# Masked scores in another pool, Q's banks read engine by engine, small copies on POOL, K copies on SP

## The chip, the core and the metric

The kernel runs on one core of one Trainium2 chip. The metric is the device time of one execution in microseconds (us); lower is better. The core has five queues that matter here: TensorE (PE; its weight loads are listed as PEld), VectorE (DVE), ScalarE (ACT), GpSimd (POOL) and SyncE (SP). Each runs its own instructions in order; across queues they wait by semaphores. DMAs are issued from POOL's queue or from SP's and carried out by 16 DMA engines.

## What is computed

Three blocks follow each other. The first is attention within chunks of 64 tokens (batch 8, 8 heads, 576 tokens, head size 64). The second mixes each token with the one before it and applies a gated two-layer network (512 to 1024 to 512). The third, the only one that the change touches, is causal attention by four experts with head size 64, of which each token takes the best two:

```
logits = x @ w_gate
topk, w = best 2 of 4 logits, softmax over these two
for e in range(4):
    q, k, v = x @ wq[e], x @ wk[e], x @ wv[e]          # (8, 576, 64)
    scores = where(causal, -1e9, q @ k.T / sqrt(64))
    a = softmax(scores)
    ye = a @ v @ wo[e]
    out += (weight of e for each token) * ye
```

## The kernel before

Every product is made from three matmuls on values split into a high and a low part (`mm3`, lines 57 to 59): high x high, high x low, low x high. High parts are rounded copies made by ScalarE, low parts the difference, made by VectorE; both read the same bank of PSUM.

The mix stage (`attn_mix`) works in units of 384 tokens. Its last unit ends with `mix_v`: the product goes through line 289 (times the gate, into `x2o`), line 46 (high half, POOL), line 292 (low half, VectorE) and line 293 (store of both, `x2T<-x2d`, POOL's queue) to memory in HBM. Its weights and buffers lie in the pools `wts` and `mx`.

The expert stage (`experts`) starts before the mix stage has ended: ahead of the last eight half products of `mix_v`, lines 768 to 794 load the first batch and make its projections; these use the pools `pX`, `wB`, `sB` (lines 469 to 472), which lie on memory that the mix stage has given back by then (`wkr`). Line 796 yields; what follows it comes later in the program. There the pools `yB`, `wB2` and `psT` are opened (lines 797 to 799): `yB` and `wB2` lie on the memory of `wts` and `mx`. The kernel's queues are put in order by a planner, which simulates the program and lets an instruction that comes earlier in the program go first where both are ready; of a pool it queues nothing ahead of the last users of the pools whose memory that pool takes.

For each batch b and pair of experts p, `p_qk` makes K and Q for both experts at once, in two halves of 288 tokens (h = 0, 1): K is split (lines 528, 529) into `Kph` and `Kpl`, and six DMAs (lines 534, 535) copy it into `K` (the high part twice, in both halves of the partitions) and `Kl`. Q is split per expert i into one tile `Q`: the high part in the expert's half of the partitions (line 518), the low part in the other half (line 519). The last 64 tokens go into `Ql` (lines 522, 523), block diagonal, so that the last, short tile of both experts runs as one. `p_v4` makes V and the gate logits of the last tile for two batches, `p_v` those of the four full tiles. All of these use two banks of PSUM in turn (tag `pj`).

A step (`t_S`, line 603) makes the scores of one tile of 128 queries into a bank (tag `S`, two banks); line 624 masks and scales them into `sm` and writes the row extreme into `nm`; line 634 takes the exponential into `P`. Three steps later `t_T` transposes `P` (line 682) and splits it into `PTh` and `PTl` (lines 688, 689, pool `wB2`); four steps later `t_AV` multiplies with V. Nine steps make a pair, 18 a batch. K and Q of the next pair are made between the steps (`fill`), in the steps 1 to 4 and 9 to 12 of a batch, and are queued behind the step's last score matmul. `t_scale` sends the row sums through HBM (lines 664 to 669, SP's queue), line 731 on POOL multiplies, line 742 splits, and `t_out` writes the output (lines 757, 760, SP's queue).

Of the kernel before, what the change touches and what calls it, by code (L numbers as in the profile page):

```python
# [8 lines left out]
F32 = mybir.dt.float32  # L9
F32R = mybir.dt.float32r  # L10
I32 = mybir.dt.int32
ACTF = mybir.ActivationFunctionType
ALU = mybir.AluOpType
# [35 lines left out]
def f32(ap):  # L49
    return ap.bitcast(F32)  # L50
# [399 lines left out]
def experts(tc, at_pool, weights, out, x2T, w_gate, wq, wk, wv, wo, ident, dram, B, S):  # L450
# [3 lines left out]
    nc = tc.nc  # L454
    E, DM, D = wq.shape
    KD = DM // 128
    EP = E // 2
    HB = S // 2
# [3 lines left out]
    LT = NT - 1  # L462
    SF = LT * 128
# [4 lines left out]
    with ExitStack() as ctx:  # L468
        px = ctx.enter_context(tc.tile_pool(name="pX", bufs=1, side="right", reuse_waits="tile"))
        wts = ctx.enter_context(tc.tile_pool(name="wB", bufs=1, side="right", reuse_waits="tile"))  # L470
        sb = ctx.enter_context(tc.tile_pool(name="sB", bufs=2, side="right", reuse_waits="tile"))
# [31 lines left out]
        def p_qk(b, p, nm, h):  # L503
            ws = w_q if nm == "Q" else w_k
            cc = slice(h * HB, (h + 1) * HB)
            pc = slice(p * 128, (p + 1) * 128)
            pp = ps.tile([128, DM], F32, tag="pj", bufs=CFG["ps"][3], name="pj")[:, :HB]
            x = x2[b]
            mm3(nc, pp, [((ws[g][0][:, pc], ws[g][1][:, pc]), (x.hi[:, g, cc], x.lo[:, g, cc])) for g in range(KD)])
            two = (b * EP + p) % 2  # L510
            if nm == "Q":
                n = min(SF, cc.stop) - cc.start
                c = slice(cc.start, cc.start + n)
                for i in range(2):
                    if h == 0:
                        Q[b, 2 * p + i] = px.tile([128, SF], F32R, tag="Q", bufs=CFG["qb"], name="Q")
                    t = Q[b, 2 * p + i]
                    nc.scalar.activation(out=t[half[i], c], in_=pp[half[i], :n], func=ACTF.Copy)
                    nc.vector.tensor_tensor(t[half[1 - i], c], pp[half[i], :n], f32(t[half[i], c]), op=ALU.subtract)
                    if n < HB:  # L520
                        d = QL[two][half[i], :, half[i]]
                        nc.scalar.activation(out=d[:, 0], in_=pp[half[i], n:], func=ACTF.Copy)
                        nc.vector.tensor_tensor(d[:, 1], pp[half[i], n:], f32(d[:, 0]), op=ALU.subtract)
                return
            if h == 0:
                K[b, p] = [px.tile([128, S], F32R, tag="Kp" + x, bufs=CFG["kp"], name="Kp" + x) for x in "hl"]
            t, l = K[b, p]
            nc.scalar.activation(out=t[:, cc], in_=pp, func=ACTF.Copy)  # L528
            nc.vector.tensor_tensor(l[:, cc], pp, f32(t[:, cc]), op=ALU.subtract)
            if h == 1:  # L530
                for i in range(2):
                    KD2[b, 2 * p + i] = d = px.tile([128, SF], F32R, tag="K", bufs=CFG["qb"], name="K")
                    for j in range(2):
                        nc.gpsimd.dma_start(out=d[half[j]], in_=t[half[i], :SF])  # L534
                    nc.gpsimd.dma_start(out=KL[two][i][half[i]], in_=l[half[i], :SF])


        V4s = [sb.tile([128, E, 2, D], F32R, bufs=1, name=f"V4{i}") for i in range(3)]
# [3 lines left out]
        def p_v4(b):  # L542

            x = sb.tile([128, 2, KD, 2, 64], F32R, tag="x0", bufs=1, name="x0")
            for i in range(2):
                for j in range(2):
                    nc.gpsimd.dma_start(out=x[:, i, :, j], in_=x2T[b // 2][i, :, j * S + SF:(j + 1) * S]
                                        .rearrange("(g p) t -> p g t", p=128))
            xh, xl = (x[:, i].rearrange("p g j t -> p g (j t)") for i in range(2))
            pp = ps.tile([128, DM], F32, tag="pj", bufs=CFG["ps"][3], name="pj")[:, :NV]  # L550
            mm3(nc, pp, [((xh[:, g], xl[:, g]), (w_v[g][0][:, :NV], w_v[g][1][:, :NV])) for g in range(KD)])
            for j in range(2):
                V4[b + j] = v = V4s[(b + j) % 3]
                G[b + j] = g = sb.tile([128, NT, E], F32, tag="lg", bufs=3, name="lg")
                r = half[j]
                pv = pp[r, :E * D].rearrange("p (e d) -> p e d", e=E)
                nc.scalar.activation(out=v[:64, :, 0], in_=pv, func=ACTF.Copy)
                nc.scalar.activation(out=v[64:, :, 0], in_=pv, func=ACTF.Copy)
                nc.vector.tensor_tensor(v[:64, :, 1], pv, f32(v[:64, :, 0]), op=ALU.subtract)
                for k in half:  # L560
                    nc.vector.tensor_copy(g[k, LT], pp[r, E * D:])

        def p_v(b, m):
            if m == 0:
                V[b] = sb.tile([128, LT, E, 2, D], F32R, tag="V", bufs=2, name="V")
            s, n = tiles[m]
            x, v = x2[b], V[b][:, m]
            pp = ps.tile([128, DM], F32, tag="pj", bufs=CFG["ps"][3], name="pj")[:, :NV]
# [34 lines left out]
        def t_S(b, p, t, i):  # L603

            s = tiles[t][0]
            nk = s + tiles[t][1]
            sm = yb.tile([128, S], F32, tag="sm", bufs=CFG["sm"], name="sm")
            nm = sb.tile([128, 2], F32, tag="nm", bufs=CFG["sm"], name="nm")
            if t < LT:
                e = 2 * p + i  # L610
# [308 lines left out]
```

## Time and profile before

| | |
|---|---|
| median of 3 runs | 1038.33 us (1037.39 to 1039.74) |
| profiled execution | 1040.81 us, its span 1038.9 us |
| mean granted TensorE clock | 0.976 of full speed |
| TensorE busy (weight loads) | 976.5 us, 94% (933.5 us, 90%) |
| VectorE, ScalarE, POOL busy | 672.6 us (65%), 577.4 us (56%), 428.1 us (41%) |
| DMA | 108.38 MB, mean 104 GB/s |

The first 120 us load the inputs and split weights; up to 656 us the mix stage keeps TensorE busy; from there to the end the expert stage runs. Busy time says when an engine had an instruction in work, the granted clock how fast TensorE was let run, and a bracket behind an instruction in a list in order of time says how long its engine was idle before it and which engine, tile and line it waited for. Matmuls overlap, so the distance of their starts, not their duration, is their pace.

### The profile page before, as it was taken

Reading aid. Unit: us, or ns where it says so; the run is one execution under the profiler, and the core shown is the slowest. Engines: PE = TensorE matmul, PEld = TensorE weight load, DVE = VectorE, ACT = ScalarE, POOL = GpSimd, SP = SyncE. Lnnn points to the kernel's source line nnn. Section 1 sums busy time; section 2 is a strip of 40 time slices with the busy share of each in tenths; the row PEclk is TensorE's granted clock in tenths of the full one; section 3 lists DMA queues with packets and bytes.
Section 4 is the critical chain, followed back from the end, with each engine's and each line's share of the span. In section 5 each row is a group of like instructions: output and inputs, shape, how many; then the busy total and the mean of one; then the engine's idle time right before and its main releaser. Section 6 shows DMA issues by size and latency. Waiting matters only on the chain.

```text
span 1038.9 us, 21755 instructions
## 1 busy us (share of the span) xinstructions
PE 976.5 (94%) x8214; PEld 933.5 (90%) x8214; DVE 672.6 (65%) x1686; ACT 577.4 (56%) x1355; POOL 428.1 (41%) x535
## 2 busy tenths in 40 slices
PE   2669899999999999999999999799999999999997
PEld 2569899999999999999999999789899899989986
DVE  5899935437654755564557432478876877877886
ACT  3478573545354645454444413266766767676665
POOL 5444303526453645464554436424342333433211
PEclk8789999999999999999999999989999999999999
DMA  8784423152324252333123124553555546353512
GB/s 223 188 198 133 118 67 82 41 122 55 90 55 110 62 122 46 98 74 91 52 52 79 35 62 117 96 154 84 163 110 151 154 95 184 74 163 72 167 32 103
DMA packets 170079, 108.38 MB, mean 104 GB/s; under 512 B 134024, under 2 KB 146424, under 8 KB 169976
## 3 DMA queue, kind: packets, MB, share of 16 engines
q1 hardware_dynamic: 132024, 54.55, 20.4%
q0 software_dynamic: 37952, 52.45, 19.6%
q8 instruction: 65, 1.06, 0.4%
q14 instruction: 38, 0.31, 0.1%
HBM read 66.01 MB, written 28.38 MB: 91 GB/s over the span
## 4 chain that ended last, share of the span: by engine, by line
PE 74%; DVE 13%; ACT 6%; DMA 3%; issue 2%; POOL 1%; SPq 1%; DVEq 0%; ACTq 0%; POOLq 0%
PE mps L57 14%; PE mps L59 13%; PE mps L58 13%; PE pj L57 6%; PE pj L59 6%; PE pj L58 6%; PE Sps L622 4%; PE Tps L127 3%; PE Tps L682 3%; PE AVps L715 2%; PE AVps L711 2%; DVE sm L624 1%; DVE PTl L689 1%; PE Sps L154 1%; DMA st<-in_moe_w_k_dram 1%
## 5 line engine op out<-in xcount | busy, mean ns | idle before, releaser
L57 PE MATMUL mps<-xhk,wkh 128*128 128x384 f32 x384 | 132.7, 347 | 2.0 <-DVE r L270 1.9
L58 PE MATMUL mps<-xlk,wkh 128*128 128x384 f32 x384 | 129.6, 338 | 0.0
L59 PE MATMUL mps<-xhk,wkl 128*128 128x384 f32 x384 | 129.4, 337 | 0.0
L57 PE MATMUL mps<-kh,wvh 128*128 128x384 f32 x384 | 129.3, 341 | 0.1
L58 PE MATMUL mps<-kl,wvh 128*128 128x384 f32 x384 | 127.7, 335 | 0.1
L59 PE MATMUL mps<-kh,wvl 128*128 128x384 f32 x384 | 126.9, 336 | 0.9 <-DVE wvl L325 0.9
L274 POOL TENSOR_TENSOR kl<-r,kh 128x384 fp32r<-128x384 f32 x80 | 86.0, 1079 | 80.4 <-ACT kh L273 80.1
L270 DVE TENSOR_TENSOR r<-mps,r 128x384 f32<-128x384 f32 x80 | 44.3, 554 | 99.9 <-ACT r L267 99.7
L634 ACT ACTIVATE P<-sm,nm 128x512 f32<-128x512 f32 (+3 forms) x144 | 83.9, 584 | 26.1 <-DVE nm L624 14.6
L228 POOL TENSOR_TENSOR xa<-XT 128x384 f32<-128x384 f32 x72 | 68.2, 955 | 62.7 <-DVE xlr L244 37.1
L624 DVE CUSTOM_DVE_ANT_0 sm<-Sps,mask 128x256 f32<-128x256 f32 (+4 forms) x160 | 74.7, 477 | 15.3 <-PE Sps L622 13.9
L689 DVE TENSOR_TENSOR PTl<-Tps,PTh 128x512 fp32r<-128x512 f32 (+2 forms) x144 | 70.7, 504 | 7.9 <-ACT PTh L688 6.9
L57 PEld LDWEIGHTS mps<-xhk,wkh 128*128 128x128 f32 x384 | 72.9, 190 | 3.0 <-DVE r L270 2.5
L242 DVE SCALAR_TENSOR_TENSOR xa<-xa,mu,XT 128x384 f32<-128x384 f32 x72 | 63.7, 900 | 15.0 <-POOL xa L228 14.9
L534 POOL DMA_DIRECT2D K<-Kph x64 | 34.5, 553 | 93.6 <-ACT Kph L528 59.2
L59 PEld LDWEIGHTS mps<-kh,wvl 128*128 128x128 f32 x384 | 71.8, 188 | 1.2 <-DVE wvl L325 1.2
L58 PEld LDWEIGHTS mps<-xlk,wkh 128*128 128x128 f32 x384 | 72.7, 189 | 0.1
L57 PEld LDWEIGHTS mps<-kh,wvh 128*128 128x128 f32 x384 | 72.0, 188 | 0.8 <-DVE x2o L289 0.4
L59 PEld LDWEIGHTS mps<-xhk,wkl 128*128 128x128 f32 x384 | 72.6, 189 | 0.0
L58 PEld LDWEIGHTS mps<-kl,wvh 128*128 128x128 f32 x384 | 72.1, 188 | 0.4 <-POOL kl L274 0.4
L273 ACT ACTIVATE kh<-r 128x384 fp32r<-128x384 f32 x96 | 50.9, 530 | 38.0 <-DVE r L270 36.9
L57 PE MATMUL mps<-xhr,wrh 128*128 128x384 f32 x192 | 66.6, 349 | 4.6 <-ACT sig L257 3.3
(188 smaller groups left out, 2855.3 us busy)
## 6 DMA issues: line engine op xcount, KB each, us to landing
x2T<-x2d POOLq DMA_DIRECT2D x48, 384.0 KB, 3.2
x<-x2T POOLq DMA_DIRECT2D x32, 576.0 KB, 6.4
ldv<-in_v_dram SPq DMA_DIRECT2D x144, 64.0 KB
ldq<-in_q_dram SPq DMA_DIRECT2D x32, 256.0 KB
ldk<-in_k_dram SPq DMA_DIRECT2D x32, 256.0 KB
K<-Kph POOLq DMA_DIRECT2D x64, 128.0 KB, 2.8
out_dram<-o SPq DMA_DIRECT2D x32, 256.0 KB
st<-in_moe_w_k_dram SPq DMA_DIRECT2D x8, 512.0 KB
```

Of the source, the lines that this page charges most:

```text
L57: nc.tensor.matmul(out=out, lhsT=ah, rhs=bh, start=first and i == 0, stop=False)
L58: nc.tensor.matmul(out=out, lhsT=ah, rhs=bl, start=False, stop=False)
L59: nc.tensor.matmul(out=out, lhsT=al, rhs=bh, start=False, stop=last and i == n - 1)
L228: nc.gpsimd.tensor_tensor(d, now, prev, op=ALU.subtract)
L242: nc.vector.scalar_tensor_tensor(a, d, m, prev, op0=ALU.mult, op1=ALU.add)
L270: nc.vector.tensor_tensor(r2, p, r, op=ALU.mult)
L273: nc.scalar.activation(out=o.hi, in_=r2, func=ACTF.Copy)
L274: eng(nc, CFG["klo"][u >= CFG["nearly"]]).tensor_tensor(o.lo, r2, f32(o.hi), op=ALU.subtract)
L622: issued = nc.tensor.matmul(out=pp[:, :w], lhsT=x, rhs=y[:, a:a + w], start=n == 0, stop=n == len(terms) - 1)
L624: nc.vector.tensor_tensor_reduce(out=sm[:, a:a + w], in0=pp[:, :w], in1=mk[:, :w], op0=ALU.add, op1=ALU.min, scale=-scale, scalar=3e38, ac ...
L634: nc.scalar.activation(out=x[:, :nk], in_=sm[:, :nk], func=ACTF.Exp, scale=-1.0, bias=nm[:, :1], accum_out=z)
L689: nc.vector.tensor_tensor(l, src, f32(h), op=ALU.subtract)
```

## The change

In the expert stage six things are done otherwise. `sm` is taken from the pool `sB` in place of `yB`. V of odd batches is taken from `yB` in place of `sB`, with one buffer in each pool in place of two in `sB`. A bank of Q is read by ScalarE for both experts and then by VectorE for both, over all its 288 columns; the tile `Q` grows from 512 to 576 columns. The remainder `Ql` is copied from `Q` by four POOL instructions in place of two by ScalarE and two by VectorE from the bank. The six copies of K are issued by SP in place of POOL. In `p_v4` the second high copy of V (line 558) and the second copy of the gate logits (line 560) go to POOL, from the first ones.

```diff
--- before.py
+++ after.py
@@ -509,18 +509,18 @@
             mm3(nc, pp, [((ws[g][0][:, pc], ws[g][1][:, pc]), (x.hi[:, g, cc], x.lo[:, g, cc])) for g in range(KD)])
             two = (b * EP + p) % 2
             if nm == "Q":
-                n = min(SF, cc.stop) - cc.start
-                c = slice(cc.start, cc.start + n)
-                for i in range(2):
-                    if h == 0:
-                        Q[b, 2 * p + i] = px.tile([128, SF], F32R, tag="Q", bufs=CFG["qb"], name="Q")
-                    t = Q[b, 2 * p + i]
-                    nc.scalar.activation(out=t[half[i], c], in_=pp[half[i], :n], func=ACTF.Copy)
-                    nc.vector.tensor_tensor(t[half[1 - i], c], pp[half[i], :n], f32(t[half[i], c]), op=ALU.subtract)
-                    if n < HB:
-                        d = QL[two][half[i], :, half[i]]
-                        nc.scalar.activation(out=d[:, 0], in_=pp[half[i], n:], func=ACTF.Copy)
-                        nc.vector.tensor_tensor(d[:, 1], pp[half[i], n:], f32(d[:, 0]), op=ALU.subtract)
+                if h == 0:
+                    for i in range(2):
+                        Q[b, 2 * p + i] = px.tile([128, S], F32R, tag="Q", bufs=CFG["qb"], name="Q")
+                ts = [Q[b, 2 * p + i] for i in range(2)]
+                for i, t in enumerate(ts):
+                    nc.scalar.activation(out=t[half[i], cc], in_=pp[half[i]], func=ACTF.Copy)
+                for i, t in enumerate(ts):
+                    nc.vector.tensor_tensor(t[half[1 - i], cc], pp[half[i]], f32(t[half[i], cc]), op=ALU.subtract)
+                if h == 1:
+                    for i, t in enumerate(ts):
+                        for j in range(2):
+                            nc.gpsimd.tensor_copy(QL[two][half[i], j, half[i]], f32(t[half[i ^ j], SF:]))
                 return
             if h == 0:
                 K[b, p] = [px.tile([128, S], F32R, tag="Kp" + x, bufs=CFG["kp"], name="Kp" + x) for x in "hl"]
@@ -531,8 +531,8 @@
                 for i in range(2):
                     KD2[b, 2 * p + i] = d = px.tile([128, SF], F32R, tag="K", bufs=CFG["qb"], name="K")
                     for j in range(2):
-                        nc.gpsimd.dma_start(out=d[half[j]], in_=t[half[i], :SF])
-                    nc.gpsimd.dma_start(out=KL[two][i][half[i]], in_=l[half[i], :SF])
+                        nc.sync.dma_start(out=f32(d[half[j]]), in_=f32(t[half[i], :SF]))
+                    nc.sync.dma_start(out=f32(KL[two][i][half[i]]), in_=f32(l[half[i], :SF]))
 
 
         V4s = [sb.tile([128, E, 2, D], F32R, bufs=1, name=f"V4{i}") for i in range(3)]
@@ -555,14 +555,14 @@
                 r = half[j]
                 pv = pp[r, :E * D].rearrange("p (e d) -> p e d", e=E)
                 nc.scalar.activation(out=v[:64, :, 0], in_=pv, func=ACTF.Copy)
-                nc.scalar.activation(out=v[64:, :, 0], in_=pv, func=ACTF.Copy)
                 nc.vector.tensor_tensor(v[:64, :, 1], pv, f32(v[:64, :, 0]), op=ALU.subtract)
-                for k in half:
-                    nc.vector.tensor_copy(g[k, LT], pp[r, E * D:])
+                nc.vector.tensor_copy(g[r, LT], pp[r, E * D:])
+                nc.gpsimd.tensor_copy(v[64:, :, 0], f32(v[:64, :, 0]))
+                nc.gpsimd.tensor_copy(g[half[1 - j], LT], g[r, LT])
 
         def p_v(b, m):
             if m == 0:
-                V[b] = sb.tile([128, LT, E, 2, D], F32R, tag="V", bufs=2, name="V")
+                V[b] = (yb if b % 2 else sb).tile([128, LT, E, 2, D], F32R, tag="V", bufs=1, name="V")
             s, n = tiles[m]
             x, v = x2[b], V[b][:, m]
             pp = ps.tile([128, DM], F32, tag="pj", bufs=CFG["ps"][3], name="pj")[:, :NV]
@@ -604,7 +604,7 @@
 
             s = tiles[t][0]
             nk = s + tiles[t][1]
-            sm = yb.tile([128, S], F32, tag="sm", bufs=CFG["sm"], name="sm")
+            sm = sb.tile([128, S], F32, tag="sm", bufs=CFG["sm"], name="sm")
             nm = sb.tile([128, 2], F32, tag="nm", bufs=CFG["sm"], name="nm")
             if t < LT:
                 e = 2 * p + i
```

## Rows read from the trace of the kernel before

**Rows 1.** Busy time by stretch: length, busy us of each engine (instructions), granted clock, DMA share, GB/s
```profile
656.50:700.00 43.50, 36.44 (x253) 34.36 (x251) 26.45 (x99) 23.82 (x68) 14.73 (x28) 0.92 0.55 135
676.50:682.30 5.80, 5.80 (x25) 5.76 (x26) 1.57 (x7) 2.62 (x8) 1.52 (x4) 0.50 0.50 144
800.00:900.00 100.00, 98.89 (x723) 93.52 (x723) 78.09 (x276) 68.61 (x198) 33.43 (x48) 1.00 0.46 121
1020.00:1038.90 18.90, 13.48 (x72) 10.17 (x70) 9.44 (x35) 8.10 (x20) 2.49 (x3) 0.96 0.27 93
```

**Rows 2.** TensorE in order of time: start, us, line, instruction, shapes, [idle before, releaser]
```profile
663.78 0.36 PE L57 MATMUL pj<-wv,x 128*128 128x260 f32 x1 [1.38 <-DVE Ql L523]
...
665.30 0.57 PE L622 MATMUL Sps<-Kl,Q 128*128 128x512 f32 x2
...
671.33 0.30 PE L58 MATMUL pj<-x,wk 128*128 128x288 f32 x1
671.46 0.29 PE L59 MATMUL pj<-x,wk 128*128 128x288 f32 x1
676.49 0.48 PE L622 MATMUL Sps<-K,Q 128*128 128x128 f32 x1 [4.74 <-DVE nm L624]
...
677.33 0.44 PE L58 MATMUL pj<-x,wk 128*128 128x288 f32 x1
677.57 0.44 PE L59 MATMUL pj<-x,wk 128*128 128x288 f32 x1
```

**Rows 3.** VectorE in order of time, around the first line 624
```profile
675.05 0.55 DVE L292 TENSOR_TENSOR x2d<-x2o,x2d 128x384 fp32r<-128x384 f32 x1
...
675.80 0.63 DVE L624 CUSTOM_DVE_ANT_0 sm<-Sps,mask 128x512 f32<-128x512 f32 x1
```

**Rows 4.** ScalarE in order of time, evictions of the first pair's Q
```profile
659.29 0.41 ACT L518 ACTIVATE Q<-pj 64x288 fp32r<-64x288 f32 x1 [0.58 <-DVE Q L519]
...
662.88 0.22 ACT L522 ACTIVATE Ql<-pj 64x64 fp32r<-64x64 f32 x1
```

**Rows 5.** By line and shape, 680 to 1040 us: count, busy us, mean ns, idle before
```profile
L534 POOL DMA_DIRECT2D K<-Kph x60 | 32.3, 553 | 90.6 <-ACT Kph L528 56.3 <-ACT PTh L688 33.2 <-issue 1.1
...
L519 DVE TENSOR_TENSOR Q<-pj,Q 64x288 fp32r<-64x288 f32 x30 | 13.7, 455 | 9.7 <-ACT Q L518 9.1
...
L518 ACT ACTIVATE Q<-pj 64x288 fp32r<-64x288 f32 x30 | 12.1, 403 | 12.7 <-PE pj L59 7.9 <-DVE Q L519 4.5
...
L522 ACT ACTIVATE Ql<-pj 64x64 fp32r<-64x64 f32 x30 | 6.5, 216 | 4.6 <-DVE Q L519 4.4
...
L742 POOL TENSOR_TENSOR Y4l<-Yf,Y4h 128x64 fp32r<-128x64 f32 x14 | 4.6, 328 | 0.1
```

**Rows 6.** Who TensorE waited for, 690 to 1000 us: total us, times, longest
```profile
PE pj L57 <- DVE Q L519: 0.9, 1, 0.9
...
PE pj L57 <- DVE Ql L523: 0.4, 1, 0.4
```

**Rows 7.** Last eviction of Q's remainder and its first use, in order of time
```profile
717.01 0.23 DVE L523 TENSOR_TENSOR Ql<-pj,Ql 64x64 fp32r<-64x64 f32 x1
...
718.17 0.39 PE L622 MATMUL Sps<-Kph,Ql 128*128 128x320 f32 x1
```

**Rows 8.** Instructions of line 46: duration ns least/median/greatest, first and last start
```profile
L46 POOL CAST wvh<-cz x8: 630/912/1812, 75.5 to 117.4; 128x512 fp32r<-128x512 f32 x8
```

**Rows 9.** POOL in order of time, the mix stage's last two stores
```profile
675.12 1.51 POOL L293 DMA_DIRECT2D x2T<-x2d  x2 [8.87 <-DVE gm L596]
```

**Rows 10.** Copies of K: time to landing, one pair's last issues, first score; stores on SP
```profile
DMA to landing us min/median/max: 2.2/2.8/3.9
...
723.14 1.07 POOL L535 DMA_DIRECT2D Kl<-Kpl  x2
...
728.31 0.42 PE L622 MATMUL Sps<-K,Q 128*128 128x512 f32 x1
...
779.67 3.46 SPq L757 DMA_DIRECT2D out_dram<-o  x2
```

## Prediction, made before the changed kernel was run

> **What bounds the kernel now.** I read the page first, then busy time by stretch, then the queues of TensorE, VectorE and ScalarE in order of time around the one long wait, and last who waits for whom in the steady part.
>
> The page says that TensorE bounds: it is busy for 94% of the span. The change takes no matmul away, so only time in which TensorE is idle or slow can be won, and the stretches say where that lies [rows 1]. From 800 to 900 us TensorE is busy 98.89 us of 100 at clock 1.00: the steady part of the expert stage offers about 1.1 us in 100. The last 18.9 us hold 5.4 us of idle time, but that is the tail of the last batch, which the change hardly touches. What stands out is the place where the mix stage ends and the expert stage begins, 656.5 to 700 us: 36.44 us busy of 43.5, and from 676.5 to 682.3 busy throughout, but at a granted clock of 0.50, the lower of the two levels (1.2 of 2.4 GHz), right after a long idle time.
>
> TensorE's queue shows that idle time [rows 2]. A matmul starts at 671.46; the next, the third group of scores, starts at 676.49 and waited 4.74 us for line 624, the masked-score eviction into `sm` and `nm`: both score banks were full. The scores in them were started by 665.30, so line 624 could have run near 666. VectorE's queue shows why it did not [rows 3]: it runs at 675.80, behind the last line 292 at 675.05 (low half of the mix stage's output). It needs no data of that. The order comes from the pools: `sm` lies in `yB`, opened on the memory of the mix stage's pools, and the planner queues nothing of such a pool ahead of the last users of the pools under it.
>
> A second, smaller wait stands before it: the projection at 663.78 waited 1.38 us for `Ql`, line 523, the last reader of a bank of Q [rows 2].
>
> **The change, part by part.** *Masked scores.* `sm` moves to `sB`, opened at line 471 on memory that is free before the last mix_v. Line 624 then depends on the scores, the mask and its own buffers, and the planner can queue it when the scores are there, up to 9 us earlier. Gone is the wait of 4.74 us. Gone with it is the slow stretch: there projection matmuls start 0.24 us apart (677.33, 677.57), against 0.13 before (671.33, 671.46) [rows 2]; of 5.8 us some 45%, 2.6 us, went to the clock. Sum 7.3 us.
>
> *Q's banks.* Now the two engines take turns on a bank: ScalarE's second copy starts at 659.29, 0.58 us after its engine came free, waiting for VectorE's first; the second half takes eight turns, and other evictions slip between, so `Ql`'s second copy runs only at 662.88 [rows 4]. Afterwards a bank takes 2 x 0.403 us on ScalarE, then 2 x 0.455 us on VectorE [rows 5]: 1.7 us with one turn between. The second half's bank would be free well before 662.40, where TensorE began to wait; the 1.38 us go, say 1.4. The Trainium skill, PSUM — Partial Sum Buffer, section "PSUM bank collisions raise a hardware error", says that two engines may use one bank at a time in different quadrants of partitions, as these halves are. By it no turns would be needed, and the new order would win nothing; the row shows that in this program they are taken.
>
> Over 16 pairs ScalarE loses 2 copies of 0.216 us each [rows 5] and its other two grow by 64 columns; VectorE the same: 5 us on each engine. In the steady part neither bounds, so this counts nothing in itself. Its upper bound is what projections wait for Q after 690 us, 0.9 + 0.4 us [rows 6].
>
> *Q's remainder by POOL.* Four copies of 64x64 per pair, which the scores of the last tile wait for. The nearest row is POOL's 128x64 subtraction, 0.328 us: 1.3 us per pair, 21 us in all, on an engine that loses 96 DMA issues of 0.553 us, 53 us [rows 5]. The cover is thin: for one pair `Ql` is complete at 717.24 and first used at 718.17 [rows 7], 0.9 us. But there too the turns go, so the bank ends sooner; I take zero. For the upper end: POOL casts of one shape took 0.63 to 1.81 us [rows 8]; stretched so, four copies take nearly 4 us, of which 0.9 us and some 2 us of sooner end are covered: about 1 us for a few of the 15 later pairs, at most 3 us in all. The Trainium skill, SBUF — State Buffer, section "Who interferes with whom", speaks against this move: a VectorE instruction with two SBUF inputs contends with a GpSimd instruction that reads SBUF. By it the sum would be that upper end; the spread of the casts agrees, though the row does not show what ran beside them.
>
> *V of the last tile and its gate logits by POOL.* Eight copies of each (in place of lines 558 and 560), first read by a product steps later: zero; were that cover gone, each would cost about what the 128x64 row has, 0.3 us, for V up to four times that by its size.
>
> *K copies by SP.* POOL loses them and with them a delay at the transition, where they stand ahead of the stores of the mix output; those end with the issue at 675.12 [rows 9], and would move up by as much as six issues, 3 us. On SP I bound an issue by POOL's 0.553 us: 3.3 us per pair beside idle time. For the transfer I take what the trace has, 2.8 us to landing [rows 10], no gain and no loss. The cover is thin here too: one pair's last copy is issued by 724.2, lands near 727.0, and its first score starts at 728.31 [rows 10], 1.3 us later.
>
> *V of odd batches in `yB`*: the same size and life, first written when the mix stage is long over: zero.
>
> **What is late next.** VectorE's 26.45 us between 656.5 and 700 [rows 1] would lie in 34.8 us instead of 43.5, 76% busy against 78% in the steady part: no bound. But the first steps must still go through eviction, exponential, transposes and their evictions. I give back 1.2 us, about the idle time of 100 steady us. So 7.3 + 1.4 - 1.2 = 7.5 us. The profiled execution took 1040.81 us with a span of 1038.9, 2.5 us above the median of the timed runs, 1038.33; the parts do not hang on this difference. **1038.3 - 7.5 = 1030.8 us.**
>
> **Rivals.** *A new wait takes the old one's place* (0.17). The transposed probabilities (`PTh`, `PTl`) still lie on the mix stage's memory, so their evictions stay behind line 292, and one of them behind the store issued at 675.12, whose two issues end at 676.6 and land, as K's do, 2.8 us later: 679.4. TensorE's work without them, from 661.8: eight groups of twelve projection matmuls at 0.13 us, 12.5 us, and four steps of scores with three transposes, some 3 us at that pace: until 677.3. It would idle 2 us and then be slow again for about as long, 2 us more: gain 3.5, **1034.8**. For it speaks that those pools don't move; against it, that the stores move up on the freed POOL queue.
>
> *K copies late* (0.07), the side that ends slower. SP runs its queue in order, and stores of the output wait there for ScalarE: two of them span 3.46 us at 779.67 [rows 10], 2.4 us more than two issues. A K copy behind such a pair eats its 1.3 us and costs TensorE 1.1 us; at every one of 15 pairs that is 16.5 us: **1047**. It outweighs the gain from a mean delay of 1.3 + 7.5/15 = 1.8 us per pair.
>
> *The order stays* (0.13): the planner queues line 624 behind line 292 as now, since all of that comes earlier in the program. Only Q's 1.4 us are won: **1036.9**.
>
> **How the numbers follow.** The forecast has 0.63, with ends of its own: 1028.3 (nothing given back, all of the 1.3 us of rows 6) and 1033.8 (the 3 us of POOL copies). The range, 1028.3 to 1036.0, takes in the first rival and leaves out the other two, 0.2. About 0.2%, 2.1 us, is what a measurement of this kernel can tell from no change. Faster by more than that: forecast and first rival, 0.80, less 0.01 for its upper end. Within: 0.13. Slower: 0.08.
>
> **What would show it.** Right: line 624 stands ahead of the last line 292 in VectorE's queue; TensorE has no wait above 2 us between 656 and 700 and keeps its clock at 1.00 there; Q's copies come in pairs and no projection waits for them; K's DMAs are in SP's queue and no first score waits for one. Wrong: a wait of transposes or products on `PTh` or `PTl` before 680 (first rival), first scores waiting for a DMA (second), a gap before the third scores as now (third). And if the steady stretches show clearly more idle time than 1 to 2 us in 100, the new order of the queues costs what the transition gives.

## The result and the profile after

The changed kernel takes **1026.41 us** in the median (1025.2 to 1027.89), the kernel before 1037.86 us beside it: a ratio of 0.9888 with a 95% interval of 0.9868 to 0.9909, or 11.4 us gained where 7.5 were forecast. The time lies 1.9 us below the forecast's range. The direction was right, and so was the sum for the transition (8.0 us in the two profiles); the forecast was too small because it gave the steady part and the tail nothing.

The profiled execution took 1027.89 us with a span of 1026.1, 1.5 us above its median (that of before lay 3 us above its own). The page's first part and the busy time of four stretches of the changed kernel (the columns are those of [rows 1]):

```profile
PE 972.5 (95%) x8214; PEld 934.0 (91%) x8214; DVE 664.5 (65%) x1646; ACT 570.0 (56%) x1315; POOL 395.6 (39%) x519
...
656.50:700.00 43.50, 41.45 (x317) 39.77 (x316) 32.92 (x121) 28.58 (x81) 13.10 (x26) 1.00 0.68 161
700.00:800.00 100.00, 97.72 (x718) 92.82 (x717) 74.16 (x260) 65.90 (x183) 28.56 (x51) 1.00 0.46 121
800.00:900.00 100.00, 98.66 (x729) 94.05 (x727) 76.13 (x271) 69.37 (x195) 26.48 (x45) 1.00 0.50 132
1007.00:1026.10 19.10, 13.11 (x70) 10.01 (x68) 9.41 (x30) 8.36 (x22) 3.06 (x3) 0.99 0.24 83
```

Against [rows 1], the stretch from 656.5 to 700 us has 317 matmuls in place of 253, and its clock is 1.00 throughout. Now look at 800 to 900 us: TensorE is busy 98.66 us where it was 98.89, which looks like no gain at all. But 729 matmuls start in it in place of 723, and the weight loads are busy 94.05 us in place of 93.52. This is the first sign of what the forecast missed.

TensorE's, VectorE's and ScalarE's queues at the transition, and whom TensorE waited for from 656.5 to 700 us (start, us, line, instruction, shapes, [idle before, releaser]; then total us, times, longest):

```profile
662.17 0.40 PE L622 MATMUL Sps<-K,Q 128*128 128x512 f32 x1
...
664.42 0.22 PE L622 MATMUL Sps<-K,Q 128*128 128x128 f32 x1
...
680.09 0.66 PE L682 MATMUL Tps<-ident,P 128*128 128x128 f32 x4 [1.02 <-DVE PTl L689]
```

```profile
659.62 0.93 DVE L519 TENSOR_TENSOR Q<-pj,Q 64x288 fp32r<-64x288 f32 x2 [1.91 <-ACT Q L517]
...
662.95 0.69 DVE L624 CUSTOM_DVE_ANT_0 sm<-Sps,mask 128x512 f32<-128x512 f32 x1 [0.80 <-PE Sps L622]
...
671.99 0.55 DVE L292 TENSOR_TENSOR x2d<-x2o,x2d 128x384 fp32r<-128x384 f32 x1
```

```profile
658.76 0.83 ACT L517 ACTIVATE Q<-pj 64x288 fp32r<-64x288 f32 x2 [4.31 <-PE pj L59]
660.34 0.84 ACT L517 ACTIVATE Q<-pj 64x288 fp32r<-64x288 f32 x2 [0.74 <-PE pj L59]
```

```profile
PE Tps L682 <- DVE PTl L689: 1.0, 1, 1.0
PE pj L57 <- DMA x<-x2T: 0.4, 1, 0.4
PE pj L57 <- PE pj L59: 0.4, 1, 0.4
PE Tps L682 <- ACT P L634: 0.2, 1, 0.2
```

The first line 624 runs at 662.95, nine microseconds ahead of the last line 292, not behind it as in [rows 3]. The third scores start at 664.42, where in [rows 2] they waited until 676.49. Q's evictions stand in pairs, two on ScalarE and then two on VectorE, and no projection waits for them (compare [rows 2, 4]). The two longest waits of the stretch, 4.7 and 1.4 us, are gone; the longest now is the 1.0 us for `PTl`.

**A ledger that busy time can't give.** The record of a matmul is longer than the step to the next one: in [rows 2] one of 128x288 lasts 0.30 us, while the next starts 0.13 us later. A start that comes late by less than the rest of that record shows as no idle time. So I went by starts. After the last matmul of mix_v every profile here has the same number of matmuls. Behind each kind and width of matmul there is a usual step to the next start (0.132 us behind a projection of 288 columns, 0.120 behind 260, 0.231 behind scores of 512, 0.108 behind a transpose). These steps add up to **346.4 us** of work in every kernel. What a step takes beyond its usual length is lost, be it a wait or a slow clock. The table counts the loss by work done, so that the same work is compared: the first 30 us of work are the transition, the last 26 the tail.

```
loss of TensorE, us      work 0-10  10-20  20-30  30-320  320-346   all   timed ratio
before                      2.3     7.8    1.3    13.5     6.8    31.7   1
changed kernel              1.0     0.0    2.4     9.6     5.5    18.5   0.9888
e1 scores                   2.6     0.0    4.0    13.5     6.9    27.0   0.9949
e2 all but scores           0.8     7.2    1.5     7.9     6.9    24.3   0.9936
e3 scores, Q                1.8     0.1    8.0     9.9     5.5    25.3   0.9943
e4 scores, K                4.7     0.1    2.1     9.9     6.8    23.6   0.9908
e5 all but K                1.2     0.8    9.5    10.9     5.5    28.0   0.9965
e6 all but Q                1.9     0.0    1.4     6.2     6.8    16.4   0.9864
e7 all but V                1.8     0.0    1.5     7.7     7.0    18.0   0.9862
e8 changed, POOL doubled    1.0     0.0    2.0    11.7     6.0    20.8   0.9895
e9 changed, POOL issues     0.8     0.1    7.6    11.7     5.0    25.3   0.9957
e10 K alone                 2.2     5.3    0.9    14.0     8.4    30.8   0.9974
e11 changed, other order    1.0     0.0    2.2     5.2     4.7    13.1   0.9839
e12 before, other order     2.3     7.3    2.0    19.5     7.9    39.0   1.0085
e13 before, second order    2.3     6.5    2.0    12.1     6.3    29.2   0.9982
e13 changed, second order   1.0     0.0    2.2     9.0     5.5    17.8   0.9871
e14 before, third order     2.3     7.9    1.3    13.2     5.7    30.3   0.9987
e14 changed, third order    1.0     0.0    2.6     8.3     6.1    18.1   0.9861
```

Of 13.2 us between the two profiles, the transition has 8.0 (11.4 to 3.4), the steady part 3.9 (13.5 to 9.6), the tail 1.3 (6.8 to 5.5). A row stands for one execution; the ratios are from all runs, each against the kernel before in the same comparison. In each of the 17 other rows the whole loss differs from that of before by what the timed ratio says, within 2 us. A loss just at an edge of two columns can fall on either side: about 1 us in e2, e5 and e7.

The Trainium skill, Trainium Kernel Development and Optimization, section "Best Practices", says that the distance to the bound is judged by the share of TensorE's peak arithmetic that is done and by the weight loads' busy share, not by the matmuls' busy share. The rows above agree in direction: from 800 to 900 us the loads gain 0.5 us while the matmuls lose 0.2. Over a longer stretch it is plainer: from 690 to 980 us the loads are busy 267.5 us before and 271.2 after, the matmuls 285.1 and 285.2.

### The profile page after: what moved, and what is told of

The parts are those of the page before. It is cut to its first block, busy times and chain, and to the rows that moved or that the text cites. A ratio compares the mean times of both kernels' runs of the same rounds, so it can differ in the third digit from the quotient of the medians.

```text
span 1026.1 us, 21849 instructions
## 1 busy us (share of the span) xinstructions
PE 972.5 (95%) x8214; PEld 934.0 (91%) x8214; DVE 664.5 (65%) x1646; ACT 570.0 (56%) x1315; POOL 395.6 (39%) x519
## 4 chain that ended last, share of the span: by engine, by line
PE 74%; DVE 12%; ACT 5%; DMA 4%; issue 2%; POOL 1%; SPq 1%; DVEq 0%; ACTq 0%; POOLq 0%
PE mps L57 14%; PE mps L59 14%; PE mps L58 14%; PE pj L57 6%; PE pj L59 5%; PE pj L58 5%; PE Sps L622 4%; PE Tps L127 3%; PE Tps L682 3%; PE AVps L715 2%; PE AVps L711 2%; PE Sps L154 2%; DVE PTl L689 1%; PE PVps L184 1%; DVE sm L624 1%
## 5 line engine op out<-in xcount | busy, mean ns | idle before, releaser
L624 DVE CUSTOM_DVE_ANT_0 sm<-Sps,mask 128x256 f32<-128x256 f32 (+4 forms) x160 | 74.2, 477 | 21.9 <-PE Sps L622 20.8
L731 POOL TENSOR_TENSOR Yf<-Yf,zb 128x576 f32<-128x576 f32 x14 | 20.0, 1430 | 153.5 <-DVE Yf L726 153.3
```

Of the source, the lines that this page charges most:

```text
L624: nc.vector.tensor_tensor_reduce(out=sm[:, a:a + w], in0=pp[:, :w], in1=mk[:, :w], op0=ALU.add, op1=ALU.min, scale=-scale, scalar=3e38, ac ...
```

## The experiments

**The parts alone.** The change was taken apart: masked scores in their own memory (with V of odd batches, which makes room), Q's banks, K's copies, and V's and the gate logits' copies by POOL. The theories were A: the steady gain comes from Q's banks; B: the masked scores win all of it; C: it comes from K's copies leaving POOL. The first kernel has this alone:

```
-            sm = yb.tile([128, S], F32, tag="sm", ...)
+            sm = sb.tile([128, S], F32, tag="sm", ...)
-                V[b] = sb.tile(..., bufs=2, name="V")
+                V[b] = (yb if b % 2 else sb).tile(..., bufs=1, name="V")
```

> Only the masked scores and V of odd batches move to other pools; Q, K and the copies stay as before. Theory A (the transition's gain is the moved scores, the steady part's gain comes from Q's banks read engine by engine): 6.5 to 8 us faster than before, near 1030.5 us; line 624 ahead of the last line 292, no long wait and clock 1.00 between 656 and 690, the 1.4 us wait on Ql still there, and after 740 us the same pace as before. Theory B (moving the scores reorders the queues and gives the steady part's 3 us as well): about 1027 us, all of the change's gain. Theory C (the steady gain is K's copies leaving POOL): as A here.

1033.35 us, ratio 0.9949 (0.993 to 0.9968). In the ledger the loss at work 10 to 20 falls from 7.8 us to nothing, close to the forecast's first term (7.3 us). But 2.7 us come back at 20 to 30, and the steady part stays at 13.5: theory B falls. What comes back stands in POOL's queue (start, us, line, [idle before, releaser]), and then in whom TensorE waits for, 670 to 690 us:

```profile
673.98 0.72 POOL L293 DMA_DIRECT2D x2T<-x2d  x1 [1.44 <-DVE c L585]
674.70 2.08 POOL L534 DMA_DIRECT2D K<-Kph  x4
676.76 1.05 POOL L535 DMA_DIRECT2D Kl<-Kpl  x2
677.77 2.95 POOL L490 DMA_DIRECT2D x<-x2T  x4
```

```profile
PE Sps L622 <- DMA K<-Kph: 1.2, 1, 1.2
```

K's copies start the moment the store of the mix output has been issued, with no idle time before them, and the loads of x right behind. In the kernel before, the same copies came later and POOL waited for ScalarE before them, so they were in nobody's way:

```profile
680.91 2.08 POOL L534 DMA_DIRECT2D K<-Kph  x4 [4.28 <-ACT Kph L528]
```

Once the scores run early, TensorE reaches the scores that read these copies sooner, and starts them 1.3 us late; the rest of the 2.7 us is spread over shorter waits.

The other three add or leave out parts in the same way: all parts but the masked scores' move; the scores and Q's banks; the scores and K's copies on SP.

> The change without its first part: scores in yB and both V in sB as before, all else as in the changed kernel. Theory A: 4 to 5 us faster than before, near 1033.5 us (1.4 us at the transition, 3 in the steady part), with the wait of line 624 and the half clock still there. Theory B: within 1.5 us of before. Theory C: as A.

1031.47 us, 0.9936 (0.9914 to 0.9958). The wait for line 624 stands as before (7.2 us lost at work 10 to 20), yet the steady part loses 7.9 in place of 13.5.

> Moved scores and V, and Q's banks read engine by engine with the remainder copied by POOL; K copies stay on POOL and p_v4 as before. Theory A: near the changed kernel, 1026 to 1028 us. Theory B: the same as with the scores alone, which is then the changed kernel's time. Theory C: as with the scores alone, near 1030.5 us.

1032.34 us, 0.9943 (0.9921 to 0.9965), no better than the scores alone. The steady part gains 3.6 us in the ledger, and the transition loses 8.0 us at work 20 to 30. As the account of the whole gain, theory A falls.

> Moved scores and V, and K's copies issued by SP; Q and p_v4 as before. Theory A: as with the scores alone, near 1030.5 us. Theory B: the same as with the scores alone, near 1027 us. Theory C: 2 to 3 us faster than with the scores alone, near 1027.5 us.

1029.06 us, 0.9908 (0.9883 to 0.9932). Of the first four this is the best, as theory C has it, though the interval takes in theory A's 1030.5 us as well. Against the scores alone the ledger gains 3.6 us in the steady part and nothing at the transition (6.9 against 6.6): in this order TensorE waits 1.5 us for the first exponential.

**One part left out.** The changed kernel with one part put back: K's copies on POOL again, Q's banks as before, or V's copies as before. Theory D: the gain behind the transition is a sum of small delays; E: K's copies alone; F: the order that the planner lays out for each kernel.

> The change without its third part: masked scores, Q's banks and the last tile's V are as in the changed kernel, K's 96 copies stay on POOL. The first four runs put K's copies on SP at about 3.5 us beside the masked scores (ratio 0.9949 without, 0.9908 with). Theory D, the gain behind the transition is a sum of small delays in the queues of VectorE, ScalarE and POOL, of which each part takes some away: ratio about 0.991 to 0.993, the stage's end some 2.5 us later than in the changed kernel. Theory E, K's copies alone won it: ratio 0.993 to 0.995, as with the masked scores alone. Theory F, any edit makes the planner lay out a new order and the rest is luck of that order: anything from 0.988 to 0.995, without relation to the part left out.

1034.8 us, 0.9965 (0.9949 to 0.9981): without K's move only 3.6 of the 11.4 us are left, less than any of the three theories had it, and all that line 624 won is lost again (9.5 us at work 20 to 30). TensorE, 670 to 690 us:

```profile
PE pj L57 <- DMA x<-x2T: 2.6, 2, 2.2
PE Sps L622 <- DVE Q L519: 2.1, 1, 2.1
PE Tps L682 <- DVE PTl L689: 0.7, 1, 0.7
```

The loads of x are not what POOL's queue holds up: they are issued 0.6 us after the last matmul that reads the old x, and 0.3 to 0.9 us after it in every profile here. What comes late is the last store of the mix output. POOL's queue, then VectorE's, then the time to landing of all 48 DMAs of line 293:

```profile
671.05 2.11 POOL L534 DMA_DIRECT2D K<-Kph  x4 [8.39 <-ACT gx L592]
...
675.13 2.90 POOL L490 DMA_DIRECT2D x<-x2T  x4
...
678.51 0.73 POOL L293 DMA_DIRECT2D x2T<-x2d  x1
```

```profile
687.86 1.35 DVE L689 TENSOR_TENSOR PTl<-Tps,PTh 128x512 fp32r<-128x512 f32 x3 [8.41 <-DMA x2T<-x2d]
```

```profile
DMA to landing us min/median/max: 2.8/3.1/9.2
```

The store stands behind K's copies and the loads of x and lands 9.2 us after its issue, where 3.1 us is usual. VectorE idles 8.4 us for it, because `PTl` lies on the mix stage's memory: this is the wait that the forecast's first rival describes. In three kernels (e3, e5, e9) the last store lands 28 to 36 us after the end of mix_v, in all others 16 to 24. The same three, and no others, have only 1.5 us of work between the last projection from the old x and the first from the new one (3.3 us or more elsewhere), so that TensorE stands while the new x lands and Q is evicted; and from 676 to 690 us the granted clock is 0.76 in e5, 1.00 in the changed kernel. That the late store makes the planner lay the work out so is the reading that fits; no run moves the store alone.

> The change without its second part: Q's banks are read in turns as before and Q's remainder is copied out of the bank by ScalarE and VectorE. The wait of 1.4 us for Q's remainder at the transition stays in all theories. Theory D: 1.4 us and 1 to 2.5 us of later delays lost against the changed kernel, ratio 0.990 to 0.992. Theory E (K's copies alone won the steady part): only the 1.4 us lost, ratio 0.989 to 0.990. Theory F: 0.988 to 0.995.

1024.79 us, 0.9864 (0.984 to 0.9888): no loss at all without Q's part. The first 10 us of work lose 0.9 us more (1.9 against 1.0), of which the projection behind `Ql` starts 0.4 us late, but the steady part loses 3.4 us less.

> The change without the copies of the last tile's V and gate logits by POOL; those two groups of eight go back to ScalarE and VectorE, some 3 us and 1.2 us of work on them in the whole stage. Theories D and E: nothing that can be measured against the changed kernel, ratio 0.988 to 0.990. Theory F: 0.988 to 0.995.

1024.38 us, 0.9862 (0.9837 to 0.9887), no loss either. The intervals of both overlap that of the changed kernel, so that either is better isn't shown, though both came out below what theories D and E had. Q's and V's parts are worth nothing that these runs can tell; the gain comes with the scores' move and K's.

**What about K's copies costs?** Two kernels tell the queue from the copy. One leaves K's copies on SP and adds as many small issues to POOL; the other moves K's copies and nothing else.

```
+                    for j in range(2):
+                        nc.gpsimd.dma_start(out=junk[b * EP + p, 3 * i + j], in_=f32(t[half[i], :16]))
+                    nc.gpsimd.dma_start(out=junk[b * EP + p, 3 * i + 2], in_=f32(l[half[i], :16]))
```

> The changed kernel, K's copies on SP as there, and beside them six DMAs per pair of heads issued by POOL after the same evictions, each of 64 rows of 64 bytes to a place in DRAM that nobody reads: POOL's queue has as many issues as with K's copies in it, the K that the scores read comes through SP. Theory P, K's copies cost because they stand in POOL's queue, ahead of the loads of x, the stores of the mix output and the product steps: the gain goes back to about what it is with K on POOL, ratio 0.993 to 0.997. Theory T, they cost because a copy issued by POOL brings K itself later (or at a later time by the planner's reckoning): ratio as the changed kernel, 0.986 to 0.990.

1032.86 us, 0.9957 (0.994 to 0.9973). Theory T falls: the K that the scores read came through SP and the time still went back by 7 us. POOL's queue and the waits, 670 to 692 us:

```profile
673.92 2.14 POOL L538 DMA_DIRECT2D junk<-Kph  x4 [5.24 <-ACT Kph L529]
676.05 1.05 POOL L539 DMA_DIRECT2D junk<-Kpl  x2
678.46 2.92 POOL L490 DMA_DIRECT2D x<-x2T  x4 [1.36 <-PE Sps L626]
681.36 0.27 POOL L524 CAST Ql<-Q 64x64 fp32r<-64x64 f32 x1
681.53 0.73 POOL L293 DMA_DIRECT2D x2T<-x2d  x1
...
682.78 0.73 POOL L293 DMA_DIRECT2D x2T<-x2d  x1
```

```profile
PE pj L57 <- DMA x<-x2T: 2.4, 3, 1.6
PE Sps L626 <- DVE Q L520: 1.4, 1, 1.4
```

An issue of 64 rows of 64 bytes keeps POOL as long as one of 64 rows of 2 KB (2.14 us for four, 2.08 above): it is the issue that costs there, not the bytes. The last two stores of the mix output now stand behind these issues and the loads of x, as in e5; the last one lands 7.7 us after its issue, at 690.5, and the first `PTh` is written at 690.7. How much of the 7 us is the delay itself and how much the other order that the planner lays out around a fuller queue isn't told apart: the order changed with it.

> The kernel before with K's copies issued by SP and nothing else. The wait of 4.7 us for the masked scores stays. Theory P, POOL's queue costs some 3.5 us in the steady part and the rest of the 7 us only where the masked scores no longer wait (there K's copies stand ahead of the loads of x): ratio 0.995 to 0.9975. If the copies cost the same with and without the masked scores' move: 0.992 to 0.994, as the kernel that has all but that move (0.9936).

1035.33 us, 0.9974 (0.9953 to 0.9994). The steady part doesn't gain (14.0), the transition gains 3.0. So theory E isn't right as it stands. K's move alone is worth 2.7 us (0.6 to 4.9), beside the scores' move 4.3 (0.9949 against 0.9908), and beside the scores', Q's and V's 8.0 (0.9965 against 0.9888). The first two can't be told apart by their intervals; the third is larger than the first. The late store comes in the three kernels in which POOL issues six DMAs per pair and copies Q's remainder too, behind scores that run early.

**VectorE held by POOL.** The trace of before shows this inside its steady part, where TensorE loses 1.25 us at one place (in order of time):

```profile
730.62 1.27 POOL L742 TENSOR_TENSOR Yl<-Yf,Yh 128x512 fp32r<-128x512 f32 x1 [1.60 <-DVE Yh L46]
...
731.09 0.83 DVE L652 TENSOR_SCALAR z<-z 128x9 f32<-128x9 f32 x1
731.22 0.40 PE L58 MATMUL pj<-wol,Yh 128*128 128x512 f32 x1
...
731.95 0.69 DVE L689 TENSOR_TENSOR PTl<-Tps,PTh 128x512 fp32r<-128x512 f32 x1
...
732.70 0.33 PE L682 MATMUL Tps<-ident,P 128*128 128x128 f32 x1 [1.08 <-DVE PTl L689]
```

Line 652 works on 128x9 numbers and takes 0.18 us in the median; here it takes 0.83 and ends within 0.04 us of POOL's line 742. Behind it stands line 689, and behind that TensorE. All such holds together, VectorE's time beyond the usual of each shape while POOL computes, come to 10.0 us before and 6.5 after. To see what a hold is worth, POOL got two more products of 128x576 behind each line 742:

```
+            if (b, p) not in direct:
+                for _ in range(2):
+                    nc.gpsimd.tensor_tensor(yf[:, c], yf[:, c], yf[:, c], op=ALU.mult)
```

> The changed kernel, and after each of POOL's 13 or 14 products steps (line 742) two more POOL multiplications of 128x576 in place on the tile Yf, which nobody reads any more: the output stays as it is. About 28 instructions of some 1.4 us. In the trace of before, VectorE instructions between tiles in SBUF that take 0.16 us otherwise took up to 0.88 us while POOL's line 742 or 731 ran, and ended with it; beyond the shortest of their form they add up to 10.6 us before and 6.9 us after. Theory L, these holds of VectorE are what the transposes wait for in the steady part: the holds grow by some 5 to 8 us and TensorE loses 2 to 4 us of it, ratio 0.991 to 0.993. Rival: POOL's work and its holds don't reach TensorE, ratio as the changed kernel, 0.988 to 0.990.

1027.91 us, 0.9895 (0.9868 to 0.9922). The holds grow by 3.5 us, to 10.0, and TensorE's loss by 2.3 us (18.5 to 20.8), 2.1 of them in the steady part. TensorE runs the same 2574 matmuls, by tile and shape, in the same sequence as in the changed kernel, so the order is not in play here; up to work 100 the ledger stays within 0.4 us of the changed kernel's. The timed ratio can't be told from the changed kernel's: the profile puts TensorE's loss at the low end of theory L's 2 to 4 us, with holds that grow less than its 5 to 8, and the time can't tell. That some of the loss comes from POOL's own work being later, and not from the holds, isn't ruled out. The Trainium skill, SBUF — State Buffer, section "Who interferes with whom", says that such VectorE instructions (two inputs in SBUF, or a form that uses both ports) and POOL's reads of SBUF shut each other out for a whole instruction. The rows agree: line 652 ended with line 742. But holds are no account of the steady gain: all but the masked scores' move has 10.7 us of them and loses 7.9 us in the steady part, less than the changed kernel does.

**How much is the order?** Every edit makes the planner lay out TensorE's queue anew. So one number of the order was moved in both kernels, with the same work on every engine: `qk1=(1, 1)` to `(2, 1)`, the projections of a batch's second pair one step of scores later.

> The changed kernel with one number of the order of work moved: the projections of K and Q of a batch's second pair of heads begin one step of scores later (2 in place of 1). No engine gets other work; the planner lays out another order (some 1,700 lines of TensorE's queue differ). Theory F, part of the differences between these kernels is the luck of such an order: the time moves by 1 to 3 us either way, ratio 0.986 to 0.992. Rival: differences are those of the queues' work alone, ratio within 0.001 of the changed kernel's.

**1020.6 us, 0.9839 (0.9818 to 0.986)**: the fastest kernel here, some 5 us under the changed one by the ratios, by an edit of one digit.

> The kernel before with the same one number moved. Theory F: the time moves by 1 to 3 us either way, ratio 0.997 to 1.003. Rival, as in the run above: within 0.001 of 1. If it comes out under 0.992, the steady part of the kernel before was poor by its order, and the change won by laying out another.

1046.15 us, 1.0085 (1.0066 to 1.0105): the same edit costs the kernel before 9 us. The two kernels in two stretches, the changed one first:

```profile
700.00:800.00 100.00, 99.56 (x735) 94.69 (x734) 76.61 (x276) 68.33 (x189) 26.96 (x50) 1.00 0.47 124
800.00:900.00 100.00, 99.73 (x729) 94.29 (x729) 76.70 (x267) 72.04 (x200) 32.05 (x53) 1.00 0.51 133
```

```profile
700.00:800.00 100.00, 97.06 (x703) 90.72 (x702) 76.84 (x275) 67.91 (x198) 39.07 (x57) 1.00 0.47 126
800.00:900.00 100.00, 98.40 (x713) 92.39 (x711) 74.02 (x263) 66.86 (x194) 34.97 (x49) 1.00 0.47 127
```

From 700 to 800 us 735 matmuls start in the one and 703 in the other, with VectorE equally busy. The steady loss goes from 9.6 to 5.2 us in the changed kernel and from 13.5 to 19.5 in the one before. After this the 3.9 us of the steady part could be mere luck. Two more orders were tried for each: `qk0=(9, 1.1)` to `(8, 1.1)`, the next batch's first pair a step sooner, and `v=(10, 0.9)` to `(11, 0.9)`, its V a step later.

> The kernel before with another single number of its order moved: the projections of the next batch's first pair begin one step of scores sooner (8 in place of 9). No engine gets other work, the transition stays. Theory O, the steady part is made by the order: ratio anywhere from 0.992 to 1.009. Theory C, the steady gain belongs to the change: ratio within 0.002 of 1.

> The changed kernel with the same number moved. Theory O: ratio anywhere from 0.982 to 0.995, the steady loss between 5 and 15 us. Theory C: 0.987 to 0.991, and 10 to 13 us under the kernel before in this order.

1036.91 us, 0.9982 (0.9964 to 1.0), and 1025.46 us, 0.9871 (0.9837 to 0.9904).

> The kernel before with the projections of the next batch's V one step of scores later (11 in place of 10). Theory O: ratio anywhere from 0.992 to 1.009. Theory C: within 0.002 of 1.

> The changed kernel with the same number moved. Theory O: ratio anywhere from 0.982 to 0.995, the steady loss between 5 and 15 us. Theory C: 0.987 to 0.991, and 10 to 13 us under the kernel before in this order.

1037.19 us, 0.9987 (0.9968 to 1.0007), and 1024.97 us, 0.9861 (0.9828 to 0.9895). In these two orders the pairs lie 11.5 and 12.2 us apart, as in the first (11.4): what theory C expects. In the order of e11 and e12 they lie 25.6 us apart. Over all four orders the steady loss is 12.1 to 19.5 us before and 5.2 to 9.6 after, with no overlap. So the change does gain in the steady part, 3 to 5 us in three orders; and one order in four moved the steady loss of either kernel by as much or more (4.4 and 6.0 us). What makes that one order good for the one and bad for the other stays open.

## Why the prediction was wrong, step by step

**Where the time lay.** Right that the transition holds the largest single loss, and that the order of the pools is its cause. The step that failed is the one by which the steady part "offers about 1.1 us in 100". The idle rows of [rows 1] and the wait rows of [rows 6] gave that bound, and both count only what sticks out behind a matmul's record. By starts, the steady part of before loses 13.5 us in 290 us of work, 4.7 in 100. A bound that was four times too tight then stood behind the forecast's zero for all of that part; measured, it went from 13.5 to 9.6 us, a gain of 3.9, and with the tail's 1.3 that is what the forecast lacked.

**Masked scores, 7.3 us.** Right: 7.8 us at work 10 to 20 went to 0.0 in the changed kernel, 7.5 over the first 20 us of work where this move stands alone. Line 624 runs when the scores are there, and the clock stays at 1.00.

**Q's banks, 1.4 us.** Right at its place: the first 10 us of work lose 1.0 in place of 2.3. As a part of the whole it brought nothing that the runs can tell, since the kernel without it is no slower.

**Given back, 1.2 us.** Right in size: the loss at work 20 to 30 rose from 1.3 to 2.4. And the reason it gave, the first steps' own chain, holds: TensorE starts 1.2 us late there for `PTl`, whose evictions stand behind Q's, and 0.6 us for x. But it stayed so small only because the DMAs had left POOL: beside the scores' move, with six issues per pair on POOL (e1, e3, e5, e9), 2.7 to 8.2 us more are lost there than before.

**K's copies by SP, zero.** The term that was mis-sized most. The forecast saw that the copies stand ahead of the stores of the mix output and that those would move up by as much as 3 us, and then counted nothing for it in its sum; it only held it against its first rival. Alone the move is worth 2.7 us, beside all else 8.0 (0.9965 without it): in e5 the last store lands late and VectorE waits 8.4 us for it. That zero was nearly right for the kernel before and wrong for the kernel after: what a queue costs has to be asked with the first wait already gone. The last store of the mix output did move up, from 676.6 [rows 9] to 673.7:

```profile
672.99 0.72 POOL L293 DMA_DIRECT2D x2T<-x2d  x1 [4.66 <-DVE nm L624]
```

**Q's remainder by POOL, zero of at most 3.** Right. A copy took 0.242 us, under the 0.328 of the nearest row, and the interference that could have made it dear cost VectorE less than 0.1 us at any one place. V's copies by POOL were right at zero too: the kernel without them is no slower.

```profile
L523 POOL CAST Ql<-Q 64x64 fp32r<-64x64 f32 x60 | 14.5, 242 | 43.0 <-ACT Q L517 36.5 <-DVE Q L519 5.1
```

**SP's price for a copy.** Bounded by POOL's 0.553 us; the bound didn't hold, it measured 0.59 in the median (56 copies from 690 us on, 0.46 to 1.38). The transfer's 2.8 us can't be checked: the trace has no landing times for SP's copies.

```profile
L534 SPq DMA_DIRECT2D K<-Kph x56: 461/588/1383, 693.1 to 986.3; - x56
```

**VectorE and ScalarE, 5 us each, "this counts nothing".** The work did go: 672.6 to 664.5 us and 577.4 to 570.0. That it counts nothing isn't borne out: of the starts more than 0.1 us late in the steady part, VectorE released 7.4 us of 10.1 before and 7.0 of 7.2 after, though it is busy only 77 to 79% of that time. Which of the small delays the change removed there, its queue's or POOL's, the runs don't settle. K's move alone removes none (14.0), the scores' alone none (13.5); the combinations of two or three parts remove 2.6 to 7.3.

**The tail, untouched.** It gained 1.3 us in the profile; the other kernels spread from 4.7 to 8.4 there, so the order of work alone can account for it.

**The rivals.** A wait on `PTl` came at 680.09, near the forecast's 679.4, but that is luck: it is 1.0 us, with no slow clock behind it, and not the rival's. The last store had landed 3.4 us after its issue, by 676.4; the evictions stand behind those of Q:

```profile
677.53 0.82 ACT L517 ACTIVATE Q<-pj 64x288 fp32r<-64x288 f32 x2 [1.19 <-PE pj L59]
678.38 1.15 ACT L688 ACTIVATE PTh<-Tps 128x512 fp32r<-128x512 f32 x3
```

```profile
678.39 0.93 DVE L519 TENSOR_TENSOR Q<-pj,Q 64x288 fp32r<-64x288 f32 x2 [0.76 <-ACT Q L517]
679.34 1.35 DVE L689 TENSOR_TENSOR PTl<-Tps,PTh 128x512 fp32r<-128x512 f32 x3
```

The rival's own wait, on the store, came where POOL's queue stayed full (e5), as the forecast's argument against it has it. No first score is seen to wait for K on SP. The order of VectorE's queue did change.

## What to carry to other kernels

Where one engine bounds, measure what it loses from the distance of its starts, against the usual distance behind an instruction of the same shape, and not from its idle time; what the rest of the program "offers" is that sum. When a long wait goes, go through every queue that runs ahead of its new end and ask what each would then delay: a queue that cost nothing behind the wait can eat all that its end won. And before a few tenths of a per cent are put down to an edit, shift the order of work by one step in both kernels; here that alone moved the time by 9 us up or 5 us down.

## What the runs showed of the hardware

A DMA issued by POOL kept its queue 0.53 us for 64 rows whether a row had 64 bytes or 2 KB. On SP the copy of rows of 2 KB took 0.59 us. A store issued by POOL right behind four loads of x landed 9.2 us after its issue in e5; the median of its line is 3.1 us. VectorE instructions of 0.2 us between tiles in SBUF took up to 0.9 us while POOL multiplied or subtracted tiles, and ended with it; POOL's short copies of 64x64 did not do that to a measurable degree. Two matmul records overlap: a record of 0.30 us with the next start after 0.13 us hides up to 0.17 us of late start.
